# Where the blocks of q and k live: a pool of their own in the room of the raw weights

## The chip, the cores and the metric

The kernel runs on one core of one Trainium2 chip. The time is device microseconds of one execution; the kernel before takes 697.77 us, the median of three runs (695.84 to 698.47). The profile is of one further execution with a span of 695.6 us. The engines are named as in the profile: PE is TensorE's matmul and PEld its weight load, DVE is VectorE, ACT is ScalarE, POOL is GpSimd and SP is SyncE; SPq is SP's queue, from which DMA transfers are issued. L136 is line 136 of the kernel before.

## The reference

Two stages follow each other. The first is linear attention with a decay per head, in blocks along the sequence; q, k and v have the shape (4 batches, 8 heads, 768 positions, 64):

```python
for b in range(nb):
    qb, kb, vb = (q[:, :, sl], k[:, :, sl], v[:, :, sl])
    intra = (qb @ kb^T * Dmask) @ vb              # lam ** (i - j) below the diagonal
    inter = (qb * lam_pow) @ kv_state
    out[:, :, sl] = intra + inter
    kv_state = lam_block * kv_state + (kb * rev_pow)^T @ vb
```

The second takes the result as 3072 tokens of 512 features:

```python
h = x @ w_in          # 512 -> 2048
g = h - np.tanh(h)
return g @ w_out      # 2048 -> 512
```

The weights come in as 64-bit floats and everything is computed in 32 bits.

## The kernel before

**Groups.** The tokens are worked off in six groups g of 512: 128 positions (BLK) of each of the four batches b. For each group the attention makes `xt`, the up projection makes the hidden tiles `g11`, `g21`, `g12`, `g22` (and a sum `gS1`), and the down projection makes the output rows. Group 0 uses plain products (`up_plain`, `down_plain`). Groups 1 to 5 use Strassen's seven products in place of eight quarter products: once for the up projection (`up(g, u, n)`, over four units u and seven products n) and for the down projection (`down`, products 1 and 2), and for the other five products of the down projection twice over, in `down_twice`, seven small products each.

**Factors in HBM.** The sums of quarters of `w_out` that the down projection needs are made while group 0 runs. `weights` brings in the raw 64-bit weights (`raw64`, pool `stage`), `round_block` rounds them with ScalarE and VectorE (L247 to L256, with the small tile `r` of the same pool) into a pair tile `wt` (pool `wst`, two of them), and `sums_out` adds the differences and writes them to HBM, as `factors` (L230, L231) and in part as `fine` (L234). At the beginning of group 1, five times four quarters are read back (`load_quarters`, L456, half of them into tiles of the ring `wb`, half into output tiles), their sums are made by VectorE (`factors_twice`, L464) and are written to `fine` (L466).

**The ring.** From then on every piece of a factor comes from HBM into the ring `wb`, seven tiles of 256 KB, in the order of use (`piece`, L475 and L478). All of these transfers are issued by GpSimd, in the order of the program.

**q, k and v.** SyncE's queue issues these loads. For groups 0 and 1 each of q, k and v is loaded in its natural order (L126), and q and k are transposed by PE (L284). From group 2 on, q and k are loaded as blocks (`load_blocks`, L136): one tile `q_blk` or `k_blk` takes 16 transfers of 16 KB each, with runs of 32 elements, so laid out that VectorE's transpose (L279) yields `qt` and `kt` at once. The blocks of one group are eight tiles (q and k of four batches); the tag `blk` has seven buffers, so the eighth waits until the first has been transposed. k is loaded a second time in natural order for the state (L314, L319), and v for the output (L350).

**Order of the work.** The tile framework orders each engine's instructions by a planner with estimated times and then inserts the waits; on the chip each engine takes its own instructions strictly in turn. VectorE's transposes, `factors_twice` and the scaling of k (L314) are held in the program's order. In group g the attention of group g + 1 is run in pieces: the transposes of batches 0 and 1 after unit 2 of the up projection, their scores after unit 3, the rest around the down projection's products; the transposes of batches 2 and 3 after the first `down_twice`. In the same VectorE queue lie the ends of the up projection (L410, hidden minus tanh, on which the down projection's matmuls wait) and L549, which makes the left operand of a later small product.

**SBUF.** Pools are stacked, in the order in which they are opened. The pools of the early part (`qpool` with the natural q, 4 KB a partition; `wst` with two pair tiles, 16 KB; `stage` with four raw tiles and two `r`, 20 KB) are closed together after group 0 by `early.close()`. One pool, `late`, then takes their room: ring tiles (14 KB), sums (8 KB), blocks (14 KB) and small tiles (3 KB), laid out by first use.

Of the kernel before, what the change touches and what calls it, by code (L numbers as in the profile page):

```python
# [9 lines left out]
F32 = mybir.dt.float32  # L10
# [6 lines left out]
BLK = 128  # L17
# [6 lines left out]
def kernel(  # L24
# [32 lines left out]
    B, H, S, D = q.shape  # L57
    NTOK, DM = out.shape
    DFF = moe_w_in.shape[1]
    NP = H // 2  # L60
# [16 lines left out]
    opool = ctx.enter_context(tc.tile_pool(name="opool", bufs=4))  # L77
    psum = ctx.enter_context(tc.tile_pool(name="psum", bufs=2, space=bass.MemoryType.PSUM))

    early = ExitStack()  # L80
    qpool = early.enter_context(tc.tile_pool(name="qpool", bufs=2))
    wst = early.enter_context(tc.tile_pool(name="wst", bufs=2))
    stage = early.enter_context(tc.tile_pool(name="stage", bufs=1))
    dram = ctx.enter_context(tc.tile_pool(name="dram", bufs=1, space=bass.MemoryType.DRAM))


# [30 lines left out]
    raw, late = {}, {}  # L117
# [11 lines left out]
    def load_blocks(g, b, names):  # L129
        for name, src in (("q", q), ("k", k)):  # L130
            if name in names:
                x = late["pool"].tile([128, NP, BLK // 32, 32], F32, name=f"{name}_blk", tag="blk", bufs=2 * B - 1)
                for p in range(NP):
                    for c in range(4):
                        blk = src[b, 2 * p + c // 2, ts(g, BLK), ts(c % 2, 32)]
                        nc.sync.dma_start(out=x[ts(c, 32), p], in_=blk.rearrange("(r t) a -> t r a", t=32))  # L136
                raw[g, b][name + "b"] = x

    def load(n):

        while at["loaded"] < min(n, len(chunks)):
            g, b = chunks[at["loaded"]]
            if g < GB:
                raw[g, b] = {}
                load_natural(g, b, "qkv")
                at["loaded"] += 1
                continue
            for b in range(B):  # L150
                raw[g, b] = {}
            nat = "kv" if g < NG - 1 else "v"
            for b in range(B - 1):
                load_blocks(g, b, "qk")
            load_blocks(g, 3, "q")
            for b in (0, 1):
                load_natural(g, b, nat)
            load_blocks(g, 3, "k")
            for b in (2, 3):
                load_natural(g, b, nat)  # L160
            at["loaded"] += B
# [53 lines left out]
    def sums_in(u):  # L215
        a11, a12, a21, a22 = (w1[u][:, 2 * c:2 * c + 2, r] for r, c in ((0, 0), (0, 1), (1, 0), (1, 1)))
        s1, s2, s4 = (ws[u][:, x] for x in range(3))
        for dst, x, y, op in ((s1, a21, a22, AL.add), (s2, s1, a11, AL.subtract), (a21, a11, a21, AL.subtract),
                              (s4, a12, s2, AL.subtract)):
            tc.keep_in_program_order(nc.vector.tensor_tensor(dst, x, y, op=op))  # L220
# [414 lines left out]
    for kt in range(KH):  # L635
# [6 lines left out]
        if kt >= KH - NU:  # L642
            sums_in(kt - KH + NU)
    early.close()
    late["pool"] = ctx.enter_context(tc.tile_pool(name="late", bufs=1))

    turns, made = (6, 11, 15, 20, 24), []
# [74 lines left out]
```

## Time and profile before

| what | value |
|---|---|
| median of three runs | 697.77 us |
| PE busy | 669.5 us, 96% of the span |
| PE's weight loads busy | 579.4 us |
| VectorE busy | 450.0 us, 65% |
| ScalarE, GpSimd busy | 194.7 us, 188.0 us |
| moved by DMA | 123.27 MB, 177 GB/s on average |
| group 1, from its second up product to that of group 2 | 155.24 to 280.91 us |
| the same of group 2 | 280.91 to 388.25 us |

The page gives each engine's busy time and, in 40 slices, where PE isn't full. The chain of work that ended last is mostly PE (79%), with DMA at 8%. The views by stage, the timelines of single engines and the waits of SyncE's queue, which are quoted below where they are used, tell what happens in one place. In a timeline, the columns are the start, the duration, engine and line, operation, tiles, the count, and in brackets the idle time just before with what ended it. In a list of waits, the columns are the time in total, the number of waits and the longest.

### The profile page before, as it was taken

How to read it: one execution, taken by the hardware profiler on the slowest of the kernel's cores; microseconds unless marked ns; L12 is line 12 of the kernel's file. 1: busy time of each engine (PE TensorE's matmuls, PEld its weight loads, DVE VectorE, ACT ScalarE, POOL GpSimd, SP SyncE). 2: the span in 40 equal slices, each digit the busy share in tenths (PEclk: the TensorE clock that was granted, in tenths of full speed). 3: DMA queues.
4: the chain of work that ended last, by engine and by line, in shares of the span. 5: the costliest groups of instructions: out<-in, count | busy, mean ns of one | idle time of the engine just before them, and what ended most of it. 6: DMA issues, size and time to landing. Idle time of an engine off the chain costs nothing.

```text
span 695.6 us, 12454 instructions
## 1 busy us (share of the span) xinstructions
PE 669.5 (96%) x4688; PEld 579.4 (83%) x4688; DVE 450.0 (65%) x786; ACT 194.7 (28%) x392; POOL 188.0 (27%) x325
## 2 busy tenths in 40 slices
PE   6999999999979869999999999999999999999998
PEld 5788755558868869888899988899988899988898
DVE  3897677984859656347777356788346786354653
ACT  2665334312311202232112233122233122233120
POOL 0001323336614414100144300243300154300262
PEclk9999999999998979999999999999999999999999
DMA  9879869669967848544598740588820366600385
GB/s 190 232 211 249 290 206 284 213 194 269 300 183 219 235 119 251 150 81 87 131 259 243 212 76 10 137 244 231 238 53 4 95 222 202 207 1 0 106 276 179
DMA packets 160427, 123.27 MB, mean 177 GB/s; under 512 B 133488, under 2 KB 133872, under 8 KB 160368
## 3 DMA queue, kind: packets, MB, share of 16 engines
q0 software_dynamic: 27504, 91.77, 41.0%
q1 hardware_dynamic: 132720, 30.71, 22.8%
q8 instruction: 37, 0.61, 0.4%
q14 instruction: 22, 0.18, 0.1%
q10 hardware_dynamic: 144, 0.00, 0.0%
HBM read 99.62 MB, written 22.81 MB: 176 GB/s over the span
## 4 chain that ended last, share of the span: by engine, by line
PE 79%; DMA 8%; issue 5%; SPq 2%; DVE 2%; POOL 2%; ACT 0%; POOLq 0%; DVEq 0%
PE y L401 16%; PE y L544 11%; PE z L401 8%; PE h L586 8%; PE zw L544 8%; PE w L506 5%; PE op L602 5%; PE y L506 5%; PE w L401 4%; PE sp L299 3%; DMA q_blk<-in_q_dram 3%; SPq L136 2%; PE op L350 2%; DMA wb<-fine 2%; PE tp L284 1%
## 5 line engine op out<-in xcount | busy, mean ns | idle before, releaser
L475 POOL DMA_DIRECT2D wb<-fine x168 | 90.4, 538 | 151.8 <-PE y L544 55.7
L478 POOL DMA_DIRECT2D wb<-factors x44 | 23.9, 545 | 188.9 <-PE y L506 177.2
L401 PE MATMUL y<-xt,w 128*128 128x256 f32 x320 | 73.2, 379 | 0.0
L401 PEld LDWEIGHTS y<-xt,w 128*128 128x128 f32 x320 | 60.5, 190 | 8.5 <-issue 0.5
L409 ACT ACTIVATE th<-g 128x512 f32<-128x512 f32 x60 | 37.8, 630 | 100.4 <-DVE g L427 40.7
L547 ACT ACTIVATE q<-y 128x128 f32<-128x128 f32 x96 | 26.6, 277 | 133.1 <-PE y L544 132.3
L544 PE MATMUL y<-wb,g 128*128 128x128 f32 x456 | 61.3, 278 | 0.0
L410 DVE TENSOR_TENSOR g<-g,th 128x512 f32<-128x512 f32 x60 | 41.4, 689 | 27.5 <-ACT th L409 27.2
L544 PEld LDWEIGHTS y<-wb,g 128*128 128x128 f32 x456 | 55.7, 192 | 1.5 <-issue 0.3
L602 PE MATMUL op<-wt,g 128*128 128x512 f32 x128 | 56.5, 595 | 0.0
L586 PE MATMUL h<-xt,w 128*128 128x256 f32 x256 | 56.1, 381 | 0.0
L586 PEld LDWEIGHTS h<-xt,w 128*128 128x128 f32 x256 | 48.3, 190 | 7.3 <-issue 0.3
L602 PEld LDWEIGHTS op<-wt,g 128*128 128x128 f32 x128 | 23.8, 190 | 27.7 <-issue 26.5
L506 PE MATMUL y<-wb,g 128*128 128x256 f32 x160 | 37.4, 393 | 5.5 <-DVE g L410 5.5
L422 DVE TENSOR_TENSOR g<-g,z 128x512 f32<-128x512 f32 x20 | 13.7, 686 | 44.4 <-ACT g L421 44.4
L544 PE MATMUL zw<-wb,g 128*128 128x128 f32 x304 | 40.2, 275 | 0.0
L506 PEld LDWEIGHTS y<-wb,g 128*128 128x128 f32 x160 | 31.4, 197 | 10.4 <-DVE g L410 5.9
L303 DVE TENSOR_TENSOR ss<-sp,mask 128x512 f32<-128x512 f32 x48 | 30.8, 682 | 13.3 <-PE sp L299 13.3
L401 PE MATMUL y<-tt,w 128*128 128x256 f32 x160 | 38.6, 385 | 0.0
L401 PE MATMUL w<-xt,w 128*128 128x256 f32 x160 | 37.8, 379 | 0.0
L401 PE MATMUL y<-tt,ws 128*128 128x256 f32 x160 | 37.8, 379 | 0.0
L401 PE MATMUL z<-tt,ws 128*128 128x256 f32 x160 | 37.8, 379 | 0.0
(125 smaller groups left out, 1231.5 us busy)
## 6 DMA issues: line engine op xcount, KB each, us to landing
wb<-fine POOLq DMA_DIRECT2D x168, 256.0 KB, 3.9
wb<-factors POOLq DMA_DIRECT2D x44, 256.0 KB, 5.4
raw<-in_moe_w_out_dram POOLq DMA_DIRECT2D x16, 512.0 KB, 5.4
v_nat<-in_v_dram SPq DMA_DIRECT2D x24, 256.0 KB, 5.0
factors<-wt POOLq DMA_DIRECT2D x8, 768.0 KB, 4.9
k_nat<-in_k_dram SPq DMA_DIRECT2D x20, 256.0 KB, 5.5
raw<-in_moe_w_in_dram SPq DMA_DIRECT2D x8, 512.0 KB, 5.2
raw<-in_moe_w_in_dram SPq DMA_DIRECT2D x16, 256.0 KB, 5.3
```

The costliest lines, as they stand in the source:

```text
L299: nc.tensor.matmul(out=sp[j][:, p, :], lhsT=kt[ts(j, 64), p, :], rhs=qt[ts(j, 64), p, :], start=True, stop=True)
L303: nc.vector.tensor_tensor(ss[:, j], sp[j], mask[:, j], op=AL.mult)
L401: nc.tensor.matmul(out=t[:, m, :], lhsT=wt[:, kt, ts(m, 128)], rhs=x[:, kt, :], start=first and m == 0 and kt == 0, stop=kt == 1, skip_gro ...
L409: nc.scalar.activation(th, src, AF.Tanh)
L410: nc.vector.tensor_tensor(dst(c), src, th, op=AL.subtract)
L475: nc.gpsimd.dma_start(out=t.rearrange("p m c -> p (m c)"), in_=fine[TWICE.index(n_), SUB.index(x_)].rearrange("p u c -> p (u c)"))
L478: nc.gpsimd.dma_start(out=t, in_=factors[XAT[FACT[n_][1]]][:, 2 * x_:2 * x_ + 2, :])
L506: nc.tensor.matmul(out=t[:, m, :], lhsT=a[:, u, kt, ts(m, 128)], rhs=wb[:, kt, :], start=first and u == 0 and m == 0 and kt == 0, stop=u = ...
L544: nc.tensor.matmul(out=dst, lhsT=a[:, u, :], rhs=wb[:, ts(u, 128)], start=x in (1, 2) and u == 0, stop=u == NU - 1, skip_group_check=True)
L547: nc.scalar.activation(keep, dst, AF.Copy)
L586: nc.tensor.matmul(out=hm[:, m, :], lhsT=w1[u][:, i, a, ts(m, 128)], rhs=xt[0, t][:, i, :], start=m == 0 and i == 0, stop=i == KI - 1, ski ...
L602: nc.tensor.matmul(out=obank[b], lhsT=g, rhs=wt[:, 2 * a:2 * a + 2, :], start=kt == 0 and a == 0, stop=kt == KH - 1 and a == 1)
```

## The change

The pool `stage` is opened before `qpool` and `wst`, and so lies at the bottom of the early room. After the early pools are closed, a pool `blk` of seven buffers is opened for the blocks of q and k, ahead of `late`. It takes the bottom 14 KB, which were the raw weights'. `late` keeps the ring, the sums and the small tiles, and so its ring begins in what is left of the raw weights' room and goes on over the natural q into the first pair tile. No operation, no transfer and no buffer count is changed; what changes is which earlier tiles a later tile has to wait for. It is for letting the blocks of group 2 be loaded as soon as the raw weights have been rounded.

```diff
+
     early = ExitStack()
+    stage = early.enter_context(tc.tile_pool(name="stage", bufs=1))
     qpool = early.enter_context(tc.tile_pool(name="qpool", bufs=2))
     wst = early.enter_context(tc.tile_pool(name="wst", bufs=2))
-    stage = early.enter_context(tc.tile_pool(name="stage", bufs=1))
     dram = ctx.enter_context(tc.tile_pool(name="dram", bufs=1, space=bass.MemoryType.DRAM))
...
-                x = late["pool"].tile([128, NP, BLK // 32, 32], F32, name=f"{name}_blk", tag="blk", bufs=2 * B - 1)
+                x = late["blk"].tile([128, NP, BLK // 32, 32], F32, name=f"{name}_blk", tag="blk")
...
     early.close()
+    late["blk"] = ctx.enter_context(tc.tile_pool(name="blk", bufs=2 * B - 1))
     late["pool"] = ctx.enter_context(tc.tile_pool(name="late", bufs=1))
```

## The prediction

> **What bounds the kernel now.** The page first: TensorE (PE) is busy 669.5 of 695.6 us, so the kernel is bound by PE, and only the 26 us in which PE stands idle, or runs at a lower granted clock, are to be had. The busy times by stage (of PE, its weight loads, VectorE, ScalarE and GpSimd, then the clock and the DMA share) say where most of them lie:
>
> ```profile
> 190.00:200.00 10.00, 10.00 (x48) 8.81 (x47) 8.84 (x15) 2.96 (x6) 3.60 (x7) 1.00 0.99 314
> 200.00:210.00 10.00, 4.49 (x20) 3.58 (x20) 2.57 (x5) 0.00 (x0) 0.54 (x1) 0.88 0.31 59
> 210.00:220.00 10.00, 10.00 (x60) 8.29 (x59) 8.55 (x15) 2.45 (x4) 5.89 (x11) 0.78 0.82 233
> ...
> 240.00:280.00 40.00, 31.48 (x323) 30.41 (x322) 21.47 (x37) 6.40 (x20) 13.91 (x26) 0.87 0.71 194
> ```
>
> Two holes, of 5.5 and 8.5 us, both while group 1 is in its down projection. After each the granted clock falls. The timeline of PE in these places, and then that of VectorE (DVE):
>
> ```profile
> 209.38 3.78 PE L506 MATMUL y<-wb,g 128*128 128x256 f32 x8 [5.51 <-DVE g L410]
> ...
> 249.66 2.04 PE L544 MATMUL zw<-wb,gS 128*128 128x128 f32 x8 [8.52 <-issue]
> ```
> ```profile
> 198.71 0.70 DVE L279 STREAM_TRANSPOSE qt<-q_blk 128x512 f32<-128x512 f32 x1
> 207.43 0.71 DVE L279 STREAM_TRANSPOSE kt<-k_blk 128x512 f32<-128x512 f32 x1 [8.03 <-DMA q_blk<-in_q_dram]
> 208.07 0.65 DVE L289 TENSOR_TENSOR qd<-qt,fwd 128x512 f32<-128x512 f32 x1
> 208.64 0.68 DVE L410 TENSOR_TENSOR g<-g,th 128x512 f32<-128x512 f32 x1
> ...
> 247.68 0.71 DVE L279 STREAM_TRANSPOSE kt<-k_blk 128x512 f32<-128x512 f32 x1 [6.78 <-DMA k_blk<-in_k_dram]
> 248.31 0.65 DVE L289 TENSOR_TENSOR qd<-qt,fwd 128x512 f32<-128x512 f32 x1
> 248.88 0.68 DVE L549 TENSOR_TENSOR gS<-gS,s 128x512 f32<-128x512 f32 x1
> ```
>
> Both holes have one cause. DVE stands in line 279 before a k block of group 2 that has not landed, and behind it in the same queue lie the operations for which PE waits: L410 (the last piece of the hidden layer) the first time, L549 (left operand of product 3) the second. That the second PE wait is called "issue" doesn't mislead: PE goes on at 249.66, 0.1 us after L549 ends at 249.56.
>
> Why do the blocks come late? The timeline of SyncE's queue (SP), then its waits up to 165 us:
>
> ```profile
> 141.80 4.30 SPq L126 DMA_DIRECT2D v_nat<-in_v_dram  x2
> 163.08 9.57 SPq L136 DMA_DIRECT2D q_blk<-in_q_dram  x16
> 172.70 11.24 SPq L136 DMA_DIRECT2D k_blk<-in_k_dram  x16
> ```
> ```profile
> SPq L136 <- DMA factors<-wt: 10.1, 1, 10.1
> SPq L136 <- DMA fine<-wt: 6.6, 2, 3.9
> ```
>
> SP is free at 146.1 but issues the first block at 163.08; it waits for the writes of `factors` and `fine` out of the last pair tile. By the sizes in the code (2 KB a partition for a block, ring tile or sum, 8 KB for a pair tile) and the order in which the pool `late` first uses its tags (ring 14 KB, sums 8 KB, blocks 14 KB), the first block's room starts 22 KB above the pool's base, and the raw weights began at 20 KB: it holds nothing of a pair tile. So the new pool as a whole waits for the release of everything beneath it. GpSimd shows the same: its first ring tile lies where q_nat was, and yet
>
> ```profile
> 163.60 2.96 POOL L456 DMA_DIRECT2D wq<-factors  x4 [3.67 <-DMA fine<-wt]
> ```
>
> **What the Trainium skill says.** "DMA: Bandwidth & Descriptors", Rules for kernel authors, advises to issue a DMA early and wait on its semaphore late; here the issue is the late part. The same page, Issuing engines are not separate DMA queues, says that DMAs of SP and GpSimd run on the same 16 engines and interleave; the trace agrees: beside GpSimd's traffic from 163 to 200 us (DMA share about 0.99) a block took SP about 10 us, with the engines less loaded (206 to 213.6) 7.7. "TensorE: Matmul & The Clock Gate", What's actually happening, says that an idle PE falls to half clock and needs about 3.4 us of work to come back; the trace agrees in kind: the eight matmuls after the first hole take 3.57 us from start to start against 1.72 for such a group before it.
>
> **The change part by part.**
> (1) Stack order. `stage` opens first, so it lies at 0 to 20 KB, q_nat at 20 to 24, the pair tiles at 24 to 40. No operation is added; nothing of the early part waits otherwise. Cost 0.
> (2) The pool `blk`, 14 KB, now opens at 0 KB: wholly within `stage`. The last reader of a raw weight or of its rounding tile is L256 at 142.91, done by 143.6. SP is then still busy with natural loads, so the first block goes out at about 146.1, some 17 us earlier. It stays in front of the same DVE operations. What hides it: from about 147.5 to 153 no DMA engine moves a byte (share 0.00 from 150 to 153), so the first q block runs at the floor of 16 issues of 0.47 us, to 153.7.
> (3) `late` without blocks (25 KB, at 14 to 39) still lies across all three old pools; ring and sums wait as before. Gain 0, cost 0 but for traffic: from 153 to 163 one more block shares the engines. From 163 to 200 the SP queue took 16.1% of 36.9 us, 5.9 us, for 54 pieces, so 16 pieces are 1.8 us of all engines. The chain pair tile, `fine`, quarters, L464 may slip by up to 2 us; DVE already idles 1.9 us there (before 171.61) with no PE idle, and from 174 to 199 has about 2 us of idle left to catch up. I take 0.
>
> Arrival of the blocks, at the 7.7 us of an easy block and 10 us of a contended one: q0 153.7, k0 163.7, q1 174, k1 184, q2 194, k2 204, q3 212, then k3, whose slot was freed by the transpose of q0 (before at 197.6), 222; with the worst block of before (14.5 us) 229; landing 2 to 4 us later. DVE asks for k1 at 199.4 at the latest: 11 us to spare. Without the first hole all later work comes about 8 us earlier, so q3 is asked for at 230.2 and L549 fits if k3 is there by 231.
>
> First hole: 5.5 idle, and then slow clock: (3.57-1.72) + (2.61-1.73) = 2.7; 8.2 us. Second hole: 8.5, and the next two groups of eight 1.84 instead of 0.89 each, scores 2.93 instead of 1.98: 2.9; 11.4 us. Sum 19.6. A check from another view: from the start of the w product of unit 0 in group 1 (155.24) to that in group 2 (280.91) are 125.7 us; from there to that of group 3 (388.25) 107.3. Both stretches hold the same PE work, so 18.3 us is what the holes cost over a good group. I take this as the most.
>
> What takes their place: the fourth factor piece of down(1,1) is issued only at 200.71, since four ring slots hold quarters, and landed 3.3 us later, at 204.0; the third piece's matmuls end at 203.86. At the 5.4 us median of such loads PE would wait 2.2 us, at 3.3 us 0.2. I take 1.0. Net 17.3, rounded to 17: 697.8 - 17 = 681.
>
> **Rivals.**
> (a) One hole stays. The natural loads stand ahead of the blocks in SP's program now; if the planner puts some behind, or k3 slips past 231, DVE waits again at 233 and about half of the second hole or all of it stays: 697.8 - 8.2 + 1 = 690.6, or 686 for half. Against it: 9 us of room by my arrivals.
> (b) No change, 696 to 699: the pool of blocks still waits for all of the early rooms, or the DMA engines, at 0.99 from 163 to 200, were the true limit and the blocks land no sooner. Against the second: the 5.5 us of empty DMA at 147.5, and only 0.31 load while DVE waited. Against the first: the new pool touches one old pool.
> (c) Slower: what the holes hid comes out. One ring piece of 256 KB is used in 0.893 us during the twofold products, which is 293 GB/s, what the engines give at best here (315 in the stages read). The ring covers 7 x 0.893 = 6.3 us against a landing of 4.4; if the blocks of group 3, now issued at 222 to 290, drive it to the 9.3 that the slowest block piece took, five turns of the ring lose 3 us each, and five cold restarts 2.8 each: 29 us against 18, some 708. For it: the blocks come while the ring runs flat out. Against it: from 345 to 390 us 70 block pieces ran beside 35 pieces of `fine` and factors, and PE idled 0.85 us in the 60 us there.
>
> **How the numbers follow.** Forecast 0.70; (a) 0.13; (b) 0.06; (c) or another slowdown, such as a different order of the planner's on DVE, 0.11. Low end 678: both holes gone with the full 19.6. High end 691: the whole of (a) at its worse end; (b) and (c), 0.17 together, lie outside. Faster by over 0.5%: 0.84; within: 0.05; slower: 0.11.
>
> **What would show it.** The first q block of group 2 is issued near 146 us instead of 163, and DMA is no longer empty from 147.5 to 153; L279 in group 1 has no DMA wait over 1 us; PE's holes at 204 and 241 shrink to under 2 us; the granted clock stays at 1.00 from 200 to 280; the w products of groups 1 and 2 are 107 to 110 us apart. Groups 2 to 5 keep their length. I am wrong if the first block still waits for `fine`, if SP puts v or k behind the blocks and the attention's matmuls wait for them, or if PE waits for ring pieces from 220 to 280.

## The result, and the profile after

The changed kernel takes 693.48 us, the median of four runs (691.42 to 693.88), beside 697.25 for the kernel before (695.84 to 698.47): a ratio of 0.9941, 95% interval 0.9912 to 0.9969. So it is faster, by about 4 us, not by the 16 to 17 that were forecast, and 693.48 lies above the range's upper end of 691. The profiled execution has a span of 692.1 us. Its lines are numbered one higher up to the pool and two higher below it (L315 is L314 of before).

The first steps came as foretold. This is the wait of SyncE's queue before its first block, and the queue's timeline (start, duration, line, tile, count):

```profile
SPq L137 <- DVE wt L257: 3.6, 1, 3.6
```
```profile
141.56 0.37 SPq L127 DMA_DIRECT2D k_nat<-in_k_dram  x1
145.90 7.47 SPq L137 DMA_DIRECT2D q_blk<-in_q_dram  x16
153.42 11.94 SPq L137 DMA_DIRECT2D k_blk<-in_k_dram  x16
165.40 12.34 SPq L137 DMA_DIRECT2D q_blk<-in_q_dram  x16
178.56 9.00 SPq L137 DMA_DIRECT2D k_blk<-in_k_dram  x16
187.60 12.64 SPq L137 DMA_DIRECT2D q_blk<-in_q_dram  x16
200.28 9.14 SPq L137 DMA_DIRECT2D k_blk<-in_k_dram  x16
209.46 13.55 SPq L137 DMA_DIRECT2D q_blk<-in_q_dram  x16
223.12 0.38 SPq L127 DMA_DIRECT2D k_nat<-in_k_dram  x1
223.91 7.63 SPq L137 DMA_DIRECT2D k_blk<-in_k_dram  x16
231.59 1.47 SPq L127 DMA_DIRECT2D v_nat<-in_v_dram  x2
233.71 15.28 SPq L137 DMA_DIRECT2D q_blk<-in_q_dram  x16
249.09 8.32 SPq L137 DMA_DIRECT2D k_blk<-in_k_dram  x15
257.51 0.38 SPq L127 DMA_DIRECT2D k_nat<-in_k_dram  x1
```

The first block waits for the last rounding step (L257) and for nothing else, and goes out at 145.90 instead of 163.08. Read on to the end: a block of group 2 takes up to 13.6 us, and the natural loads have moved. Before the change, the k of batch 2 and the v of batches 2 and 3 of group 2 were issued ahead of the first block (the two v from 141.80 on). Now the k stands behind seven blocks, at 223.12, the two v stand behind eight, at 231.59, and the k of batch 3 comes last of all, at 257.51.

What PE makes of it, in its timeline:

```profile
207.47 1.97 PE L507 MATMUL y<-wb,g 128*128 128x256 f32 x8 [0.42 <-DVE wt L465]
...
235.79 1.16 PE L545 MATMUL zw<-wb,s 128*128 128x128 f32 x8 [0.83 <-DMA wb<-fine]
...
239.22 1.13 PE L545 MATMUL zw<-wb,gS 128*128 128x128 f32 x8 [1.24 <-DVE gS L550]
...
261.20 1.01 PE L320 MATMUL kv<-v_nat,k_nat 128*64 128x64 f32 x14 [8.13 <-DVE k_nat L315]
```

The hole of 5.5 us has gone (0.42 is left), that of 8.5 has shrunk to 1.24, and a new one of 8.1 us has opened at 253, in the attention of group 2, before the second half of the state's matmuls (14 of these 16 fall into the window of this view). VectorE tells what is missing there:

```profile
237.23 0.71 DVE L280 STREAM_TRANSPOSE kt<-k_blk 128x512 f32<-128x512 f32 x1 [2.76 <-DMA v_nat<-in_v_dram]
...
260.46 0.69 DVE L315 TENSOR_TENSOR k_nat<-k_nat,mask 128x512 f32<-128x512 f32 x1 [11.49 <-DMA k_nat<-in_k_dram]
```

(The first line names v as the releaser, but in the generated program the transpose waits for the k block alone; the profile infers releasers.) The natural k of batch 3 was issued at 257.51 and landed at 260.4. The busy times by stage (columns as in the prediction) show where the holes went:

```profile
200.00:210.00 10.00, 9.58 (x45) 8.15 (x44) 10.00 (x18) 1.76 (x3) 5.03 (x10) 1.00 0.72 217
...
250.00:260.00 10.00, 3.07 (x76) 2.76 (x68) 0.00 (x0) 1.08 (x2) 0.51 (x1) 0.91 0.56 140
260.00:280.00 20.00, 18.80 (x146) 18.24 (x147) 11.62 (x21) 3.37 (x11) 9.56 (x17) 0.87 0.74 205
```

The account of group 1, from its w product (157.48) to group 2's (277.95): 120.5 us, against 125.7 before and 107.3 for a good group. The difference from a good group is made up of 0.8 us of PE idle at the read back quarters (a wait for ScalarE's L422), the four holes above, 10.6, and about 2.0 of slow clock after the last (1.87 and 1.35 us for two groups of eight matmuls at 0.89, and 0.5 in L320): 13.4 together, where 13.2 was measured. So group 1 won 5.2 us. Group 1 also began 2.2 us later than in the profile before, and what follows it is 0.5 us shorter: 5.2 - 2.2 + 0.5 is the 3.5 us between the two spans.

### The profile page after: what moved, and what is told of

Its sections match the earlier page's. It is cut to its first block, busy times and chain, and to the rows that moved or that the text cites. A ratio compares the mean times of both kernels' runs of the same rounds, so it can differ in the third digit from the quotient of the medians.

```text
span 692.1 us, 12452 instructions
## 1 busy us (share of the span) xinstructions
PE 666.6 (96%) x4688; PEld 576.8 (83%) x4688; DVE 449.9 (65%) x786; ACT 194.4 (28%) x392; POOL 188.0 (27%) x325
## 4 chain that ended last, share of the span: by engine, by line
PE 75%; DMA 11%; SPq 5%; DVE 5%; issue 2%; POOL 1%; ACT 0%; POOLq 0%; DVEq 0%; ACTq 0%
PE y L402 16%; PE y L545 10%; PE z L402 8%; PE h L587 8%; PE zw L545 7%; SPq L137 5%; PE op L603 5%; PE y L507 4%; PE w L507 4%; PE w L402 4%; DMA k_blk<-in_k_dram 3%; DMA q_blk<-in_q_dram 3%; PE sp L300 2%; PE op L351 2%; DMA wb<-fine 2%
## 5 line engine op out<-in xcount | busy, mean ns | idle before, releaser
L545 PE MATMUL y<-wb,g 128*128 128x128 f32 x456 | 62.2, 280 | 0.0
L545 PEld LDWEIGHTS y<-wb,g 128*128 128x128 f32 x456 | 56.6, 194 | 1.5 <-issue 0.3
L545 PE MATMUL zw<-wb,g 128*128 128x128 f32 x304 | 40.6, 277 | 0.0
L402 PE MATMUL z<-xt,ws 128*128 128x256 f32 x160 | 37.8, 379 | 0.0
L545 PEld LDWEIGHTS zw<-wb,g 128*128 128x128 f32 x304 | 37.5, 194 | 0.0
```

The source lines that it names most:

```text
L402: nc.tensor.matmul(out=t[:, m, :], lhsT=wt[:, kt, ts(m, 128)], rhs=x[:, kt, :], start=first and m == 0 and kt == 0, stop=kt == 1, skip_gro ...
L545: nc.tensor.matmul(out=dst, lhsT=a[:, u, :], rhs=wb[:, ts(u, 128)], start=x in (1, 2) and u == 0, stop=u == NU - 1, skip_group_check=True)
```

## The experiments

**Theory after the result.** Both holes that are left, at the last k block and at the natural k, come from SyncE's queue, which takes its loads strictly in turn. The buffer of the natural k of batch 3 (three buffers for four batches) is freed by L320 at 225.8 us. In the generated program its load stood behind 7 block transfers of group 3 before the change; now it stands behind 31, since the planner, with the blocks of group 2 out of the way earlier, lets those of group 3 go ahead. SyncE's queue differs from before by four places only, those of this load and of the three natural loads that went behind the blocks of group 2; every other engine has the same instructions in the same order. Rival: it isn't the order but the load on the DMA engines.

**Which part of the change does it: two runs with one part each.** First the pool of blocks without the new order of the pools, so that the blocks lie over the natural q and the pair tiles:

```diff
-    stage = early.enter_context(tc.tile_pool(name="stage", bufs=1))
     qpool = early.enter_context(tc.tile_pool(name="qpool", bufs=2))
     wst = early.enter_context(tc.tile_pool(name="wst", bufs=2))
+    stage = early.enter_context(tc.tile_pool(name="stage", bufs=1))
```

> The pool of blocks is kept, but the raw weights' pool is opened last again, so the blocks lie over the natural q and the pair tiles; no engine's order differs from the kernel before. Theory (a pool waits for the whole of every old pool that it touches): the first q block, which lies over a natural q alone, still goes out only after the last write of fine, near 163 us, and the time is that of the kernel before, 697. Rival (a tile waits only for what lay in its own bytes): first block at about 146 us, time as for the changed kernel or less, 690 to 694.

Measured: 0.9999 of the kernel before (0.9976 to 1.0022), first block at 163.89 us. Then the new order of pools without the pool of blocks:

```diff
-                x = late["blk"].tile([128, NP, BLK // 32, 32], F32, name=f"{name}_blk", tag="blk")
+                x = late["pool"].tile([128, NP, BLK // 32, 32], F32, name=f"{name}_blk", tag="blk", bufs=2 * B - 1)
...
-    late["blk"] = ctx.enter_context(tc.tile_pool(name="blk", bufs=2 * B - 1))
```

> The raw weights' pool is opened first, but the blocks stay in the one late pool; no engine's order differs from the kernel before. Theory: first block near 163 us, 697 us, both holes of the kernel before present. Rival for the start of the changed kernel, which was 2.2 us later at the beginning of group 1: if the place of the raw weights' tiles makes their loads slower, group 1 begins 2 us later here too and the time is 699; if it was one execution's chance, group 1 begins at 153.5 us within 1 us.

Measured: 0.9995 (0.9977 to 1.0013), first block at 163.75. The w product of group 1, from which its account starts, begins at 155.89; the expectation counts from the first up product, 1.7 us earlier, so 154.2. Neither part alone does anything that can be told from the noise. With the pool alone, a block that lies over a natural q alone still waits for the pair tiles: a pool waits for all of each old pool that it touches, as the prediction took it.

**The changed kernel once more.**

> The changed kernel unchanged, for a second profile. Theory: again 693, with a hole of about 8 us in group 1 before the second half of L320 that waits for a natural k. The 2.2 us by which group 1 began later: if it comes from the change, it is there again; if by chance, group 1 begins anywhere from 153 to 156 us.

Measured: 692.41 us, 0.9909 of before (0.9881 to 0.9938). Group 1's w product begins late again, at 157.81 (156.1 as the expectation counts). The holes are there, but differently shared out:

```profile
242.25 2.04 PE L545 MATMUL zw<-wb,gS 128*128 128x128 f32 x8 [4.74 <-issue]
...
261.38 1.12 PE L320 MATMUL kv<-v_nat,k_nat 128*64 128x64 f32 x16 [3.28 <-DVE k_nat L315]
```

Here the last k block came 3 us later (its last piece was issued by 235.25, and VectorE went on at 240.27), and PE lost 4.7 us there. It therefore reached the natural k later and waited less. 1.24 + 8.13 in the first profile, 4.74 + 3.28 in this one: what is lost at the block is saved at the natural k, because the latter comes at a time of its own (256 to 257.5). The forecast of "about 8 us" for the one hole holds only for the two together.

**The natural k from another queue.**

```diff
-                nc.sync.dma_start(out=x, in_=src[b, :, ts(g, BLK), :].rearrange("h s d -> s h d"))
+                eng = nc.scalar if (name, g, b) == ("k", GB, 3) else nc.sync
+                eng.dma_start(out=x, in_=src[b, :, ts(g, BLK), :].rearrange("h s d -> s h d"))
```

> One load of the changed kernel, the natural k of batch 3 in group 2, is issued from ScalarE's queue instead of SyncE's; nothing else differs. Theory (place in SyncE's queue: that load stands behind 31 block transfers of group 3): it goes out within 2 us of the matmuls that free its buffer (at 225.8 us), lands by 235, and PE's hole of 8.1 us before the second half of L320 is gone, with some 2 us of slow clock: about 10 us under the changed kernel, 683. Rival (the DMA engines are so loaded by the ring and the blocks that it lands late from any queue): it lands after 250 us and most of the hole stays, 691 to 694. A second rival: the hole goes and another of the same size opens in group 1, 691 to 694.

Measured: 703.42 us, 1.0057 of before (1.0041 to 1.0074), slower than both, which no theory had expected. ScalarE's timeline:

```profile
248.45 0.39 ACTq L128 DMA_DIRECT2D k_nat<-in_k_dram  x1
249.01 0.28 ACT L549 ACTIVATE q<-y 128x128 f32<-128x128 f32 x1 [24.96 <-DMA k_blk<-in_k_dram]
```

The load did not go out at 226 but at 248.45. In the generated program the loads of SyncE's and ScalarE's queues share eight completion counters, dealt out in the planner's order, and each load first waits for the one before it on its counter; for this load that is a k block of group 3. So it kept its place in the order, on another queue, and ScalarE stood still for 25 us while PE waited 23.1 us for ScalarE. The run is therefore no test of the place in the queue. What it does tell: issued at 248.45, the load landed 3.3 us later, among the blocks and the ring. The time from issue to landing is not where the 30 us go, which speaks against the rival.

**The order of issue alone.** The blocks of group 3 are queued behind that load; no wait is added:

```diff
+                natk[name, g, b] = nc.sync.dma_start(out=x, ...).ins
...
+            with tc.issue_after(natk["k", GB, 3]) if g == GB + 1 else nullcontext():
-            for b in range(B - 1):
-                load_blocks(g, b, "qk")
-            load_blocks(g, 3, "q")
+                for b in range(B - 1):
+                    load_blocks(g, b, "qk")
+                load_blocks(g, 3, "q")
```

> In the changed kernel, the blocks of group 3 are queued behind the natural k of batch 3 of group 2 (order of issue alone, no wait added); every other engine's order is unchanged. Theory (place in SyncE's queue): that load goes out near 234 us and lands by 240, so the hole before the second half of L320 (8.1 us in the first profile of the changed kernel, 3.3 in the second) is gone; the other hole, before the k block of batch 3, may stay at 1 to 5 us: 685 to 688, 5 to 8 under the changed kernel. Rival (the DMA engines' load): the natural k is late all the same, 691 to 694.

Measured: 685.59 us, 0.9819 of before (0.9782 to 0.9856). The natural k goes out by 239 and the hole at L320 is gone. In the generated program that load's place is the only difference in any engine's order from the changed kernel, so it was the order that made this hole. At the block 3.25 us are left (L546 and L551 are L545 and L550 of the changed kernel):

```profile
236.86 2.16 SPq L127 DMA_DIRECT2D k_nat<-in_k_dram  x1
```
```profile
241.24 2.05 PE L546 MATMUL zw<-wb,gS 128*128 128x128 f32 x8 [3.25 <-DVE gS L551]
```

**The block out of the way alone.** Batch 3 of group 2 is transposed one product later:

```diff
-        run(p1[0:1])
+        run([(att_transpose, 2, (2,))] if g == 1 else p1[0:1])
...
-        run(p1[1:2])
+        run([(att_transpose, 2, (3,)), (att_scores, 2, (2,))] if g == 1 else p1[1:2])
...
-        run(p1[2:])
+        run([(att_scores, 2, (3,))] * (g == 1) + p1[2:])
```

> In the changed kernel, batch 3 of group 2 is transposed after product 5 instead of after product 4, with its scores after product 6, so that L550 no longer stands behind a k block that has not landed; the natural k is left where it is. Theory: PE's hole inside product 4 is under 0.5 us, but PE then reaches the natural k sooner and waits longer there, 8 to 11 us, since that load still goes out near 257: no gain, 691 to 694. Rival (the k block is the true limit): 688 or less.

Measured: 691.51 us, 0.9898 (0.9861 to 0.9935), that is, the changed kernel's time. The block's hole is gone and the other takes the whole:

```profile
258.65 1.12 PE L320 MATMUL kv<-v_nat,k_nat 128*64 128x64 f32 x16 [8.61 <-DVE k_nat L315]
```

**Both.**

> Both of these. Theory: neither hole of group 1 is left over 1.5 us; what stays is some 1 us at the read back quarters, 0.5 at the fourth piece and 0.8 at a ring piece. From the w product of group 1 to that of group 2 109 to 112 us instead of 120.5, and 682 to 685. Rival (the ring then runs short of DMA): new waits of PE for ring pieces from 225 to 280 us of 3 us and more, 687 or more.

Measured: 680.46 us, 0.9756 of before (0.9723 to 0.9788), 1.5 us under the range that was expected, with 108.3 us from group 1's w product to group 2's. All that PE still waits in group 1:

```profile
205.02 1.96 PE L508 MATMUL y<-wb,g 128*128 128x256 f32 x8 [0.37 <-DVE wt L466]
...
248.12 0.98 PE L352 MATMUL op<-ss,v_nat 128*64 128x128 f32 x13 [0.16 <-DVE ss L305]
```

It is the version that beats both kernels. A second set of runs:

> The changed kernel with order and split again, on the same chip, beside the same runs of the kernel before: 679 to 683, with no hole over 1.5 us in group 1.

Measured: 681.68 us, 0.9765 (0.9724 to 0.9806). Beside the same two short waits, PE waits 1.1 and 0.9 us for ring pieces here, no more.

**The same two edits without the change of pools.**

> The two edits of the run with order and split, on the kernel before: the pools are as they were, so the blocks of group 2 still go out only after the last write of fine. Theory: the first hole of the kernel before (5.5 us before the fourth piece of the first down product, with 2.7 us of slow clock) stays, since the k block of batch 1 is as late as before; the second (8.5 us and 2.9) is gone or under 3 us: 686 to 690, so that the pool itself is worth 6 to 9 us beside the other two edits. Rival (the two edits were the whole gain and the pool adds nothing): 680 to 683.

Measured: 693.03 us, 0.9935 of before (0.9908 to 0.9963), 3 us above the expectation. The first hole is there in full, and the second is not as small in effect as was expected:

```profile
209.76 3.78 PE L508 MATMUL y<-wb,g 128*128 128x256 f32 x8 [5.41 <-DVE g L412]
252.12 2.05 PE L546 MATMUL zw<-wb,g 128*128 128x128 f32 x8 [3.06 <-issue]
```

3.06 us of idle brought the slow clock with it (0.66 on average from 250 to 260). So the pool alone gives about 5 us (0.9941 and 0.9909), the two edits without it about 4.5, and all three together 16 to 17: each takes away only a part of what holds up the same chain.

## Why the prediction was wrong

- **Right: what bounds the kernel, and part (2).** The pool as a whole waits for what lies under it. 0.4 us were left of the first hole where 1.0 had been taken, and the clock is at 1.00 from 200 to 250. That the first block went out at 145.9, as foretold (146.1), is luck. The prediction had SP busy with the natural v until then; in the changed program those loads stand behind the blocks, SP was free at 141.9, and the block waited for the last rounding step, which came 2.2 us later than in the profile before.
- **Right: the size of the prize.** "I take this as the most" gave 18.3 us over a good group. With order and split 17.4 of them are regained (125.7 to 108.3), and 680.46 is the time forecast for the change alone.
- **Wrong: when the last k block arrives.** The sum took the second hole as gone because k3 would be issued by 222, or at the worst block's 14.5 us by 229, and land 2 to 4 us later. It was issued by 231.5 and 235.3 in the two profiles, and its slowest piece took 5.8 and 6.1 us to land. VectorE, which stood free for it from 234.5 and 234.4 on, went on at 237.2 and 240.3. In the first profile 9.5 us were lost up to the issue. The five blocks from k0 to k2, put at about 10 us each, took 9.0 to 12.6, which with a wait of 0.8 between them is 5.7 us too much. q3, put at 8 us after the "easy block", took 13.6: another 5.6. The other way, k3 with the natural k before it took 1.5 us less than the 10 put down, and q0 ended 0.3 us sooner.

The easy block was read between 206 and 213.6, where the DMA share was 0.38. GpSimd, which issues the ring's loads, stood still there until 210.22, for a step of VectorE that lay behind the late k block of the first hole:

```profile
210.22 0.54 POOL L466 DMA_DIRECT2D fine<-wt  x1 [8.96 <-DVE wt L464]
```

Take the hole away and that quiet goes with it: in the changed kernel the share from 206 to 213.6 is 0.90. So this price came from a stage that the change abolishes. What makes a block slow can be read from the waits of SP's queue between 100 and 300 us in the changed kernel:

```profile
SPq L137 <- DMA q_blk<-in_q_dram: 11.5, 13, 2.2
SPq L137 <- DMA k_blk<-in_k_dram: 10.6, 16, 1.8
```

With eight counters a load waits until the eighth before it has landed, so the 16 pieces of a block take either their 16 issues, 7.5 us, or about two landings. The pieces of the easy block landed in 1.7 us (median), those of the blocks from 153 to 223 in 3.7 to 5.7. This is a rough reading (13.6 us went with a median of 4.2, 9.1 us with one of 4.5), and no run varied it.

- **Wrong: what else stands in SP's queue.** The sum had nothing for it. Rival (a) named it ("if the planner puts some behind") and gave it 0.13, but charged one hole, 690.6, and the signs of being wrong name a v or k put behind the blocks. Both conditions of (a) came true: natural loads went behind the blocks, and k3 slipped past 231. The natural k of batch 3, which can't go before 225.8, was overtaken by 31 transfers of group 3. In the first profile this is 8.1 us and 2.0 of slow clock, of the 12.2 that group 1 took beyond the forecast's 108.3 (107.3 and the 1.0 for the ring). The two wrong steps share one delay, so the runs divide it differently: by the ratios, order alone regained about 7 us over the changed kernel and the split another 4 on top, while the split alone regained little (0.9898, beside 0.9909 and 0.9941). The trace of before held the sign of it: there too this load stood behind transfers of group 3, but only 7, and it landed at 252.8, 9 us before VectorE used it, after two holes.
- **Perhaps too light: part (3)**, which took 0 for the quarters' delay. PE lost 0.8 us there in one profile of the changed kernel and nothing in the other, but also 0.3 us in the profile with the two edits and the old pools. How much of it is the pool's isn't shown.
- **Did not come true: (c).** The ring cost PE at most 1.1 us at one place.
- **Small slips, on which nothing hangs.** The DMA engines are empty only from 150 to 153 us (from 147.5 to 150 the share is 0.35). The 0.85 us of idle PE in (c) belong to the 45 us from 345 to 390. Half of the second hole in (a) gives 684.9 by its own terms and not 686.
- **Open: the start of group 1**, 2.2 us later in the changed kernel's profile. It goes back to raw weights that land later at about 24 us. The run with the new pool order alone has the same instructions, addresses and waits up to there as the changed kernel, and begins group 1 at 155.89, which speaks for chance. But the second profile of the changed kernel begins it late again, and by the expectation for that run, which gave chance 153 to 156, its 156.1 (from the first up product) speaks for the change. The w product of group 1 begins in the seven profiles of kernels with the early blocks between 156.0 and 158.9 and in the four without between 155.2 and 156.0, which chance alone would seldom do. What makes it differ was not found; if it is the change's doing, it costs some 1.5 us, the difference of the two means.

## What to carry to other kernels

When a queue is served in turn, moving one load forward moves everything that the planner can now put behind it: list what stands between a load and its last possible time on that queue, before and after, not only the load that was moved. Take the price of a transfer from a stage that will still exist after the change; a quiet stretch next to a stall can be a product of the stall, as it was here. And where several late inputs feed one chain, taking away one of them shows little until the others are gone: here the pool gave about 5 us without the two edits, these 4.5 without the pool, and all three over 16.

## What the runs showed of the hardware

After idle times of 3.06 us (the two edits on the old pools), 3.25 us (order alone) and more in group 1, the next eight small matmuls took 1.8 to 1.9 us instead of 0.9; after 1.24 us (the changed kernel) they took 1.0. One and the same program shared 8 to 9 us of idle time quite differently between two holes in two profiled executions (693.84 and 693.68 us), so a single profile does not give the size of one hole to better than a few us.
